# Inverse-spectral tables of a two-layer S5/H3 kernel: TensorE and PSUM copies in place of two transposing DMA transfers, with a new written order

## The chip, the cores and the metric

The kernel runs on one core of a Trainium2 chip. The metric is the device time of one execution in microseconds. A profiled execution gives a trace of its own; its span (first to last instruction) is some two microseconds shorter than the device time of the same execution. Engines are named as in the profile: PE (TensorE matmuls), PEld (its weight loads), DVE (VectorE), ACT (ScalarE), POOL (GpSimd) and SP (the queue that issues nearly all transfers).

## The reference, cut to what matters

A sequence `x` of 2048 tokens with 640 channels goes through four residual layers, A, B, A, B. The two A layers share their weights, and so do the two B layers.

```
x = x + A(layernorm(x)); x = x + B(layernorm(x))      # and the same two once more
A(x): h[t] = lam * h[t-1] + Bbar x[t]   (complex diagonal, 640 states)
      y = 2 Re(C h) + x * Dskip
B(q): k_shift = causal convolution of k with 4 taps;  kv = k_shift * v
      y = irfft(rfft(kv) * rfft(ssm_k))[:2048] + kv * ssm_D      # per channel, length 4096
      returns q * y
```

In layer B only `q` depends on `x`. So `y` of layer B, the long convolution, is computed once from the inputs and used twice.

## The kernel before, in words

**Convolution.** It is a transform of length 4096 written as matmuls with tables of sines and cosines. The 640 channels are taken in five blocks of 128, `yq0` to `yq4`. Each block has these steps, which are the names in the written order:

- `kl`, `ka`, `KA`, `KB`: load the filter, add the skip term, first stage (four groups `m0` to `m3` of matmuls, L1098, each with a copy `e0` to `e3` out of PSUM) and second stage (five groups, L1122 to L1127, with the tables `Cf`, `Sf` and `NSf`);
- `vl`, `VA`, `VB`: the same two stages for `kv`, which `kv_lk`, `kv_lv`, `kv_mm` (L1062) and `kv_ev` (L1068) make;
- `pw`: the pointwise complex product of the two spectra, four DVE instructions (L1175 to L1178);
- `IB`: the first inverse stage, five groups of matmuls (L1197, L1198) with the tables `Ci`, `Si` and `NSi`, each with a copy;
- `tt`: a transposing transfer from arena to arena (L1210); `IA`: the second inverse stage (L1225); `st`: the store to the DRAM scratch `ysd`.

**Tables.** `yt_sin` makes `Cf` and `Sf` on ACT (three groups of up to six of the 17 frequencies, 128 columns each), `yt_neg` makes `NSf`. The inverse tables hold the same blocks, each of them transposed: `yt_Ci` and `yt_Si` are one transposing transfer each (L882, issued by SP) of 17 blocks of 128x128 bf16, and `yt_nsi` negates `Si` on DVE (L886).

**A layers.** Four chunks `c0` to `c3` of 512 tokens each, in each of `A1` and `A2`. Per chunk: layernorm (`ln_bn` for A1, `ln_nm` and `ln_sq` for A2), normalised rows `id`, a transposing transfer `tu`, input products `bq` (L658) and `bp` (L673, L675) with copies `eq` and `ev`, rotation `ri` (L690, L691), two scans `sc` (L707), carry `cy`, rotation back `ro`, `hx` (L732), output products `cp` (L755, four per chunk) and their copies with the residual, `xe` (L763 on ACT for A1, L767 on DVE for A2). The B layers have per chunk a load `l` of `ysd`, layernorm, `u`, a product `mm` (L812) and a sum `m` (L818, L820); the last one stores the output, `st` (L783). The weights of A are made by the `a_` steps.

**Order.** Each step is a task. The string `ORDER` lists all tasks, and `Sched.run` emits them in this order; each engine then works through its own instructions in that order and waits by semaphores for what they need. A suffix `/a`, `/d` or `/p` gives the engine, ACT, DVE or POOL, of a step that has a choice. `evac` (L254 on ACT, L256 on DVE) is the copy out of PSUM. The table `PLACE` gives every buffer its offset in one arena of SBUF and every PSUM tile its first bank out of eight; a buffer that overlaps an older one waits for the older one's last reader.

Of the kernel before, what the change touches and what calls it, by code (L numbers as in the profile page):

```python
# [51 lines left out]
ARENA = 3216  # L52

ORDER = """
    warm yt_io6 kv_kd a_ldB1 a_pl kv_pd1/p kv_pd3/p kv_pd2/p yt_io0 yt_ph6 yt_f0 kv_dsl yt_ph0 yt_sin6 a_ldB0 yt_io12 kv_pd0/p yt_f2 yq0_kl yt_ph12
    yt_sin0 a_p0 kv_d0 a_b01:3 kv_k0 kv_lk0 a_b00:2 a_b0e1:3/d kv_k1 a_b00:3 a_b0e0:2/d kv_d1 yt_f3 a_b0e0:3/a kv_k2 a_p1 yt_f4 a_b00:4 yt_sin12 a_p2
    a_b01:2 kv_lv0 yt_neg6 a_ti a_b01:4 yt_h0 yq0_ka a_b0e1:2/d kv_d2 a_b0e1:4/d yq0_KA:m2 kv_ds0 yq0_KA:m3 a_b0e0:4/a yq0_KA:e2/d yq0_KA:m1 a_p3 yq1_kl
    yq0_KA:m0 kv_ds1 yt_neg12 kv_mm0:0 yt_neg0 yq0_KA:e1/a yq0_KA:e0/d kv_ds2 yq0_KA:e3/a a_p4a kv_lv1 a_p4 a_b00:1 a_p5a yq0_KB:m1 a_b0e0:1/a kv_ds3
    kv_ev0:0 a_ta kv_mm0:1 yq0_KB:e1/d kv_ds4 yq0_KB:m4 kv_lk1 a_b00:0 yq1_ka kv_ev0:1 a_p5b yq0_KB:m0 yt_h1 a_b0e0:0/d yq0_KB:m2 yq0_vl yq0_KB:e4/a a_t0
    yq0_KB:e0/a a_b01:0 a_b01:1 yq0_KB:e2/a a_b0e1:1/a a_p6 a_ldC0 a_t1 a_b0e1:0/d kv_mm1:1 a_lamd kv_mm1:0 a_ldC1 kv_ev1:1 a_b10:1 kv_ev1:0 yq0_VA:m2  # L60
    yq0_KB:m3 a_b1e0:1/d yt_Si yq0_VA:m3 yq0_VA:e2/a yq0_KB:e3/d yq1_KA:m1 yq0_VA:e3/a yq0_VA:m0 yq1_KA:e1/d a_b11:4 yq0_VA:e0/a yq0_VA:m1 yq1_KA:m2
    a_b1e1:4/a yq0_VA:e1/d a_b10:4 yt_Ci yq1_KA:e2/a yq1_KA:m3 yq0_VB:m3 a_b1e0:4/a yq1_KA:e3/d yt_h2 yq0_VB:m0 yq0_VB:e3/a yt_h3/p yq1_KA:m0 a_b10:0
    yq0_VB:e0/d yq1_KA:e0/a yq0_VB:m1 yq1_vl a_f a_b1e0:0/a a_ct1 yq0_VB:e1/a yq0_VB:m2 yt_nsi a_wc01:0 a_b11:0 kv_lk2 yq0_VB:m4 a_wm01:0 a_b1e1:0/a
    yq0_VB:e2/d a_wc01:1 a_b11:3 yq0_VB:e4/a xl0 a_wm01:1 a_b1e1:3/a yq1_KB:m2 yq0_pw yq1_KB:m3 yq1_KB:e2/a yq1_KB:m0 kv_lv2 yq1_KB:e3/a yq1_KB:m1
    yq1_KB:e0/a a_b10:2 a_b11:1 yq1_KB:e1/a a_b11:2 kv_lk3 a_b1e1:1/a a_b10:3 a_b1e1:2/a yq1_VA:m3 kv_pd4/p a_b1e0:3/a kv_mm2:1 yq1_VA:e3/a kv_lv3
    yq1_VA:m0 a_b1e0:2/a kv_ev2:1 yq0_IB:m3 yq1_VA:e0/a yq0_IB:m0 yq0_IB:e3/d kv_mm2:0 yq0_IB:e0/a yq2_kl yq1_VA:m2 yq0_IB:m1 kv_ev2:0 yq1_VA:e2/a
    yq0_IB:m4 yq0_IB:e1/a A1c0_ln_bn:2/d yq1_VA:m1 yq2_vl a_ct0 yq1_VA:e1/a yq0_IB:e4/d yq0_IB:m2 A1c0_ln_bn:0/d a_wc00:0 yq1_VB:m0 a_t2 yq1_KB:m4
    a_wm00:0 yq1_VB:e0/a yq0_IB:e2/d a_wc00:1 yq1_VB:m1 yq1_KB:e4/a A1c0_ln_bn:3/a a_wm00:1 yq0_tt kv_mm3:0 yq1_VB:e1/d a_ct4 kv_ev3:0 a_ct2 a_wc04:0
    a_wc02:0 a_wm04:0 yq1_VB:m3 a_wm02:0 a_wc04:1 a_wc02:1 a_wm04:1 yq1_VB:e3/a a_wm02:1 yq1_VB:m2 yq2_ka kv_lv4 yq2_KA:m3 yq2_KA:m0 yq1_VB:e2/d kv_mm3:1
    yq2_KA:e3/a yq2_KA:e0/a yq1_VB:m4 yq2_KA:m2 kv_ev3:1 a_dd yq1_VB:e4/a yq2_KA:e2/a yq2_KA:m1 kv_lk4 yq1_pw yq2_VA:m2 yq2_KA:e1/a yq2_VA:m3 yq2_VA:e2/a  # L70
    xl2 yq2_VA:e3/a yq2_VA:m0 yq2_KB:m0 yq2_VA:e0/a yq2_KB:m2 yq2_KB:e0/a a_ct3 yq2_KB:e2/a yq2_KB:m4 yq3_kl yq0_IA:m0 a_wc03:0 yq2_KB:m1 yq0_IA:e0/a
    a_wm03:0 yq2_KB:e1/a yq1_IB:m3 yq3_vl yq2_KB:e4/d a_wc03:1 A1c0_ln_bn:1/d yq1_IB:m4 kv_mm4:1 yq1_IB:e3/a a_wm03:1 yq1_IB:e4/a yq1_IB:m1 kv_ev4:1
    yq2_VA:m1 yq0_IA:m1 yq1_IB:e1/a yq2_VA:e1/d yq4_kl yq1_IB:m2 yq1_IB:m0 yq0_IA:e1/d yq1_IB:e2/a yq2_VB:m1 yq1_IB:e0/d A1c0_ln_sd kv_mm4:0 yq3_ka
    yq2_VB:e1/d yq1_tt yq2_VB:m0 kv_ev4:0 yq2_KB:m3 yq2_VB:e0/a yq2_VB:m2 A1c0_ln_post yq2_KB:e3/a A1c2_ln_bn:1/d yq2_VB:m3 yq2_VB:e2/a A1c0_id:3/d
    yq2_VB:m4 yq3_KA:m1 A1c0_id:2/d yq2_VB:e3/a yq2_VB:e4/d yq3_KA:m2 A1c0_id:0/d yq3_KA:m3 yq3_KA:e1/a A1c0_id:1/d yq3_KA:m0 yq2_pw A1c0_tu yq3_KA:e2/a
    yq3_VA:m2 yq3_KA:e3/a yq3_KA:e0/a yq1_IA:m0 yq3_VA:e2/a yq3_KB:m4 yq0_st yq1_IA:m1 yq1_IA:e0/a yq3_KB:m1 yq1_IA:e1/a yq3_KB:m3 xl1 yq3_KB:e1/a
    yq3_VA:m3 A1c0_bq:2 yq3_KB:e4/a yq3_KB:e3/a yq3_VA:e3/d yq2_IB:m2 yq1_st A1c0_eq:2/a A1c2_ln_bn:3/d yq2_IB:m4 yq2_IB:m3 yq2_IB:e2/a yq2_IB:e4/d
    yq2_IB:m1 A1c2_ln_bn:2/d yq2_IB:e3/a yq4_vl yq3_VA:m1 yq3_KB:m0 A1c1_ln_bn:2/d yq2_IB:e1/a yq2_IB:m0 yq3_VA:e1/a A1c1_ln_bn:1/d yq3_KB:m2 yq2_IB:e0/a
    A1c2_ln_bn:0/d A1c0_bp:2 yq3_KB:e2/a yq2_tt A1c1_ln_bn:3/d A1c2_ln_sd yq3_VA:m0 A1c0_bq:1 A1c0_ev:2/a A1c2_ln_post yq3_KB:e0/a A1c2_id:3/d yq4_ka
    A1c1_ln_bn:0/d yq3_VA:e0/a yq4_KA:m3 A1c2_id:1/d yq4_KA:m0 A1c0_eq:1/a yq3_VB:m2 yq4_KA:e3/d yq4_KA:e0/a yq3_VB:m1 A1c2_id:2/d A1c2_id:0/d A1c1_ln_sd  # L80
    yq3_VB:e2/a yq3_VB:m3 A1c2_tu yq3_VB:e1/d yq3_VB:m0 A1c1_ln_post yq3_VB:m4 A1c0_bp:1 yq3_VB:e0/a A1c1_id:2/d A1c1_id:0/d yq3_VB:e4/d yq3_VB:e3/a
    A1c1_id:3/d xl3 A1c1_id:1/a yq3_pw yq4_KA:m1 A1c0_bq:0 A1c0_ev:1/a A1c1_tu yq4_KA:e1/a yq4_KA:m2 A1c2_bq:2 A1c0_eq:0/a yq2_IA:m1 A1c0_bp:0 yq2_IA:e1/a
    yq4_KA:e2/a A1c2_eq:2/d yq2_IA:m0 A1c0_xr A1c0_ev:0/a yq3_IB:m1 yq2_IA:e0/a A1c2_bp:2 A1c0_ri yq3_IB:e1/a A1c1_bq:0 A1c2_ev:2/a yq4_KB:m2 yq3_IB:m3
    A1c0_sc yq4_KB:e2/a yq3_IB:m2 yq3_IB:e3/a yq4_KB:m3 A1c1_eq:0/a A1c1_bq:1 yq3_IB:e2/a yq4_KB:e3/a yq3_IB:m4 yq4_KB:m1 A1c1_eq:1/a yq3_IB:e4/d
    yq3_IB:m0 A1c3_ln_bn:1/a yq4_KB:e1/d A1c1_bq:2 A1c3_ln_bn:3/d A1c2_bq:0 yq3_IB:e0/a A1c0_cy A1c0_ro A1c1_eq:2/a yq3_tt yq4_KB:m4 yq4_KB:m0 A1c2_eq:0/a
    A1c1_bp:0 yq4_KB:e0/a yq4_KB:e4/d A1c1_bp:2 A1c3_ln_bn:2/d A1c1_ev:0/a yq4_VA:m2 yq4_VA:m0 yq2_st A1c1_ev:2/d A1c1_bp:1 yq4_VA:e0/a A1c3_ln_bn:0/d
    yq4_VA:e2/a yq4_VA:m1 yq4_VA:m3 A1c1_ev:1/d A1c2_bp:0 yq4_VA:e1/a A1c1_ri yq4_VA:e3/a A1c2_bq:1 A1c2_ev:0/a A1c3_ln_sd yq4_VB:m3 A1c2_eq:1/a A1c0_hx
# [748 lines left out]
def y_table_tasks(S, nc, wp, St, consts):  # L836
# [43 lines left out]
    for a, b in (("Ci", "Cf"), ("Si", "Sf")):  # L880
        def e_tr(_, a=a, b=b):
            nc.sync.dma_start_transpose(out=T[a].get(), in_=T[b].get().rearrange("p q k -> p (q k)"))  # L882
        t_tr.append(S.add(f"yt_{a}", "sp", 3.5, sins, e_tr, xt=2.8, uses=[T[a], T[b]]))

    def e_nsi(_):
        nc.vector.tensor_scalar(T["NSi"].get(), T["Si"].get(), -1.0, None, ALU.mult)  # L886
# [494 lines left out]
```

## Time and profile before

| what | value |
|---|---|
| median of 3 runs | 350.53 us (350.0 to 350.71) |
| the profiled execution as a run | 350.02 us |
| its span | 348.2 us |
| PE busy | 310.0 us (89%) |
| DVE busy | 326.5 us (94%) |
| ACT busy | 256.3 us (74%) |
| DMA, mean over the span | 120 GB/s; 20 transposes from arena to arena, 5 from DRAM |

Busy time is the time in which at least one instruction of the engine is shown as running; since instructions overlap at their ends, it is less than the sum of their durations. A group of instructions is given with its line, engine and shapes, its count, its busy time with the mean duration of one, and the engine's idle time just before them with what ended it. Lines are those of the kernel before.

### The profile page before, as it was taken

Reading aid. Unit: us, or ns where it says so; the run is one execution under the profiler, and the core shown is the slowest. Engines: PE = TensorE matmul, PEld = TensorE weight load, DVE = VectorE, ACT = ScalarE, POOL = GpSimd, SP = SyncE. Lnnn points to the kernel's source line nnn. Section 1 sums busy time; section 2 is a strip of 40 time slices with the busy share of each in tenths; the row PEclk is TensorE's granted clock in tenths of the full one; section 3 lists DMA queues with packets and bytes.
Section 4 is the critical chain, followed back from the end, with each engine's and each line's share of the span. In section 5 each row is a group of like instructions: output and inputs, shape, how many; then the busy total and the mean of one; then the engine's idle time right before and its main releaser. Section 6 shows DMA issues by size and latency. Waiting matters only on the chain.

```text
span 348.2 us, 9466 instructions
## 1 busy us (share of the span) xinstructions
PE 310.0 (89%) x4110; PEld 248.4 (71%) x4110; DVE 326.5 (94%) x449; ACT 256.3 (74%) x411; POOL 20.6 (6%) x62
## 2 busy tenths in 40 slices
PE   7777897779799999999999999999999999998910
PEld 7665887768698899896666786876877787654500
DVE  8999898899999989798999999999999999999996
ACT  6999898797998768566867689897776856008850
POOL 5690000010000000000000000000000000000000
PEclk9999999899999999999999999999999999999975
DMA  8999999887999920800259642315009500000024
GB/s 231 218 170 257 186 228 154 167 185 152 180 230 179 218 77 10 174 2 0 77 120 215 189 177 52 100 18 130 6 5 227 135 15 2 0 2 0 3 112 188
DMA packets 105868, 41.71 MB, mean 120 GB/s; under 512 B 98141, under 2 KB 100706, under 8 KB 105826
## 3 DMA queue, kind: packets, MB, share of 16 engines
q1 hardware_dynamic: 105680, 41.10, 53.7%
q8 instruction: 32, 0.52, 0.6%
q14 instruction: 10, 0.08, 0.1%
q10 hardware_dynamic: 146, 0.01, 0.0%
HBM read 19.02 MB, written 5.24 MB: 70 GB/s over the span
## 4 chain that ended last, share of the span: by engine, by line
PE 62%; DVE 27%; ACT 6%; issue 3%; POOL 0%; DVEq 0%; ACTq 0%; POOLq 0%
PE banks L755 18%; PE banks L658 11%; PE banks L673 11%; ACT arena L254 5%; DVE arena L256 3%; DVE arena L690 3%; DVE arena L707 3%; DVE arena L820 3%; DVE arena L767 3%; PE banks L1197 2%; PE banks L1198 2%; PE banks L675 2%; PE banks L1098 2%; PE banks L1289 2%; PE banks L1122 2%
## 5 line engine op out<-in xcount | busy, mean ns | idle before, releaser
L254 ACT ACTIVATE arena<-banks 128x1024 bf16<-128x1024 f32 (+4 forms) x150 | 129.5, 929 | 31.9 <-PE banks L658 9.2
L755 PE MATMUL banks<-arena 128*128 128x128 bf16 (+1 forms) x800 | 101.0, 283 | 1.7 <-DVE arena L767 1.7
L755 PEld LDWEIGHTS <-arena 128*128 128x128 bf16 x800 | 60.6, 98 | 41.7 <-issue 1.9
L673 PE MATMUL banks<-arena 128*128 128x256 bf16 x400 | 53.2, 273 | 0.0
L256 DVE CAST arena<-banks 128x1024 bf16<-128x1024 f32 (+4 forms) x43 | 41.7, 979 | 5.6 <-PE banks L675 2.5
L658 PE MATMUL banks<-arena 128*128 128x256 bf16 x400 | 46.2, 273 | 0.0
L690 DVE TENSOR_TENSOR arena<-arena 128x5160 bf16<-128x5160 bf16 x16 | 45.5, 2844 | 0.4
L707 DVE TENSOR_TENSOR_SCAN arena<-arena 128x1290 bf16<-128x1290 f32 x16 | 44.7, 2833 | 0.3
L673 PEld LDWEIGHTS <-arena 128*128 128x128 bf16 x400 | 38.6, 98 | 4.6
L658 PEld LDWEIGHTS <-arena 128*128 128x128 bf16 x400 | 38.5, 98 | 4.7
L555 ACT ACTIVATE junk<-arena,nmean 128x640 bf16<-128x640 f32 x48 | 39.7, 827 | 1.3
L1122 PE MATMUL banks<-arena 128*128 128x128 bf16 x170 | 35.5, 221 | 4.6 <-DVE arena L427 1.5
L1125 PE MATMUL banks<-arena 128*128 128x128 bf16 x170 | 35.7, 221 | 0.0
L1127 PE MATMUL banks<-arena 128*128 128x128 bf16 x150 | 33.2, 221 | 0.0
L1124 PE MATMUL banks<-arena 128*128 128x128 bf16 x150 | 33.2, 221 | 0.0
L609 ACT ACTIVATE arena<-arena,nmr,rstd 128x640 bf16<-128x640 f32 (+1 forms) x32 | 27.8, 912 | 5.8 <-DVE nmr L568 3.8
L691 DVE TENSOR_TENSOR arena<-arena 128x2580 bf16<-128x2580 bf16 x16 | 24.1, 1504 | 0.5
L675 PE MATMUL banks<-arena,ident_bf 128*128 128x256 bf16 x80 | 21.8, 273 | 0.0
L763 ACT ACTIVATE arena<-banks 128x640 f32<-128x640 f32 x15 | 10.4, 697 | 14.0 <-PE banks L755 14.0
L1197 PE MATMUL banks<-arena 128*128 128x128 bf16 x160 | 19.6, 219 | 0.7 <-ACT arena L254 0.5
L1198 PE MATMUL banks<-arena 128*128 128x128 bf16 x160 | 19.4, 219 | 0.3 <-DVE arena L1178 0.3
L1124 PEld LDWEIGHTS <-arena 128*128 128x128 bf16 x150 | 14.8, 99 | 5.1 <-issue 5.1
(196 smaller groups left out, 498.8 us busy)
## 6 DMA issues: line engine op xcount, KB each, us to landing
arena<-in_A_x_dram SPq DMA_DIRECT2D x8, 640.0 KB, 5.5
arena<-ysd SPq DMA_DIRECT2D x8, 640.0 KB, 5.9
arena<-in_B_ssm_k_dram SPq DMA_DIRECT2D x5, 512.0 KB, 7.7
arena<-in_B_v_dram SPq DMA_DIRECT2D x5, 512.0 KB, 6.3
ysd<-arena SPq DMA_DIRECT2D x5, 512.0 KB, 4.5
out_dram<-arena SPq DMA_DIRECT2D x8, 320.0 KB, 2.2
arena<-in_A_B_im_dram SPq DMA_DIRECT2D x1, 800.0 KB, 5.2
arena<-in_A_B_re_dram SPq DMA_DIRECT2D x1, 800.0 KB, 7.1
```

The lines of the kernel that those rows point to most:

```text
L254: nc.scalar.activation(out, in_, ACT.Copy)
L256: nc.vector.tensor_copy(out, in_)
L555: nc.scalar.activation(small.junk, src(q), ACT.Square, bias=st["nmean"][:, i:i + 1], scale=1.0, accum_out=st["ssq"][:, i:i + 1])
L658: nc.tensor.matmul(pq[:, jj, c2, :], lhsT=bt0[:, c2, k, j * P:(j + 1) * P], rhs=uT[:, 2:4, k, :], start=(k == 0), stop=(k == NJ - 1))
L673: nc.tensor.matmul(pb[:, jj, c2, :], lhsT=bt1[:, c2, j, k, :], rhs=uT[:, 0:2, k, :], start=(k == 0), stop=False)
L690: nc.vector.tensor_tensor(tt, gs[:, :, None].to_broadcast([P, 2, 2, n]), by_pairs(w["tab"].get().rearrange("p i j b -> p (i j b)"), n), AL ...
L707: nc.vector.tensor_tensor_scan(gv, rt, gv, 0.0, ALU.mult, ALU.add)
L755: nc.tensor.matmul(pc[:, o0:o1], lhsT=lh, rhs=rh, start=(n == 0), stop=(n == len(ops) - 1))
L1122: nc.tensor.matmul(ps[:, g, 0, :], lhsT=T["Cf"].get()[:, q, :], rhs=are, start=True, stop=single)
L1124: nc.tensor.matmul(ps[:, g, 0, :], lhsT=T["Sf"].get()[:, q, :], rhs=A[:, 2 * q + 1, :], start=False, stop=True)
L1125: nc.tensor.matmul(ps[:, g, 1, :], lhsT=T["NSf"].get()[:, q, :], rhs=are, start=True, stop=single)
L1127: nc.tensor.matmul(ps[:, g, 1, :], lhsT=T["Cf"].get()[:, q, :], rhs=A[:, 2 * q + 1, :], start=False, stop=True)
```

## The change

`yt_Ci`, `yt_Si` and `yt_nsi` go. In their place stand fifteen smaller tasks. For `Cf` and for `Sf`, the 17 blocks are taken in groups of 8, 8 and 1. Each group is multiplied by the identity, block by block, with the block as weights, so that the transposed blocks stand in PSUM (`yt_tCf0`, `yt_tCf8`, `yt_tCf16`, the same for `Sf`; 34 matmuls in all). From there `Ci` (from `Cf`), `Si` and, with a factor of -1, `NSi` (both from `Sf`) are copied to the arena by ACT or DVE (`yt_eCi0` and so on, nine copies of 1024, 1024 and 128 columns). What needed the three old steps needs all nine copies.

`ORDER` is written anew throughout, with the same other tasks; 80 steps that have a choice of ACT or DVE stand on the other one than before, and three small memsets go from POOL to DVE. `PLACE` is new throughout as well, with places in PSUM for the six new tiles, and the arena is 3212 units in place of 3216. The new tasks stand in the order together, after yq1's `KB:e0` and before yq0's `IB`:

```
... yq1_KB:e0/a yt_tCf8 kv_lk3 a_b10:2 a_b1e1:2/a yt_tSf0 yt_eCi8/a yt_tSf8 yt_eNSi0/a a_b1e0:2/d xl0
yt_eSi0/a yt_eNSi8/d yt_tCf0 kv_mm2:0 yt_eCi0/a yt_eSi8/d yt_tSf16 yt_tCf16 kv_lv3 yt_eNSi16/a yq1_VA:m3
yt_eCi16/d yt_eSi16/a kv_ev2:0 yq1_VA:m0 kv_mm2:1 yq1_VA:e3/a yq1_VA:e0/a yq1_VA:m2 yq0_IB:m3 ...
```

The diff of the code, without `ORDER` and `PLACE`:

```diff
-    t_tr = []
-    for a, b in (("Ci", "Cf"), ("Si", "Sf")):
-        def e_tr(_, a=a, b=b):
-            nc.sync.dma_start_transpose(out=T[a].get(), in_=T[b].get().rearrange("p q k -> p (q k)"))
-        t_tr.append(S.add(f"yt_{a}", "sp", 3.5, sins, e_tr, xt=2.8, uses=[T[a], T[b]]))
-
-    def e_nsi(_):
-        nc.vector.tensor_scalar(T["NSi"].get(), T["Si"].get(), -1.0, None, ALU.mult)
-    K["inv"] = t_tr + [S.add("yt_nsi", "dve", 0.65, t_tr, e_nsi, uses=[T["NSi"], T["Si"]])]
+    inv = []
+    for b, outs in (("Cf", (("Ci", 1.0),)), ("Sf", (("Si", 1.0), ("NSi", -1.0)))):
+        for g0 in range(0, NQ, 8):
+            n = min(8, NQ - g0)
+            s_pt = S.bank(f"it{b}{g0}", (n + 3) // 4)
+
+            def e_tm(_, b=b, g0=g0, n=n, s_pt=s_pt):
+                for q in range(n):
+                    nc.tensor.matmul(s_pt.get()[:, q * P:(q + 1) * P], lhsT=T[b].get()[:, g0 + q, :], rhs=consts["ident_bf"][:], start=True, stop=True)
+            t_tm = S.add(f"yt_t{b}{g0}", "pe", c_mm(P, n), sins, e_tm, uses=[s_pt, T[b]])
+            for a, sc in outs:
+                def e_te(eng, a=a, sc=sc, g0=g0, n=n, s_pt=s_pt):
+                    o, i = T[a].get()[:, g0:g0 + n, :].rearrange("p q k -> p (q k)"), s_pt.get()[:, 0:n * P]
+                    if eng == "act":
+                        nc.scalar.activation(o, i, ACT.Copy, scale=sc)
+                    else:
+                        nc.vector.tensor_scalar(o, i, sc, None, ALU.mult)
+                inv.append(S.add(f"yt_e{a}{g0}", ("act", "dve"), (c_act(n * P), c_tt(n * P, True)), [t_tm], e_te, uses=[s_pt, T[a]]))
+    K["inv"] = inv
```

## The prediction

> **What bounds the kernel now.** I read three views in this order: busy time by stretch, the timeline around the two places where the stretches change, and the groups of instructions by shape. First the stretches. The columns are PE, PEld, DVE, ACT and POOL busy time with the number of instructions, then the granted clock, the DMA share and GB/s.
>
> ```profile
> 10.00:43.20 33.20, 24.87 (x606) 21.93 (x604) 31.74 (x58) 32.06 (x52) 13.77 (x38) 1.00 1.14 206
> 43.20:98.40 55.20, 45.92 (x1084) 41.59 (x1082) 51.24 (x64) 47.98 (x62) 1.83 (x5) 0.97 0.93 179
> 98.40:281.90 183.50, 183.50 (x1933) 144.96 (x1933) 173.04 (x221) 141.31 (x238) 0.00 (x0) 1.00 0.46 109
> 281.90:332.00 50.10, 48.16 (x409) 32.35 (x407) 49.51 (x58) 24.58 (x43) 0.00 (x0) 1.00 0.03 10
> 332.00:348.20 16.20, 0.00 (x0) 0.00 (x0) 12.87 (x22) 3.81 (x12) 0.00 (x0) 0.61 0.35 133
> ```
>
> There are three regimes. Up to 98.4 us DVE and ACT carry the load (DVE 91 to 96% busy) and PE has holes. From 98.4 to 281.9 us PE has no hole, while DVE leaves 10.5 us empty. From 281.9 us DVE is full to the end, and after 332 us it is alone. The chain of waits says the same: PE pieces from 98.38 (L658) to 281.11 us, then DVE pieces only. The second view shows the joints.
>
> ```profile
> 25.74 10.76 SPq L882 DMA_TRANSPOSE arena<-arena  x2
> 94.46 0.64 PE L1225 MATMUL banks<-HA,arena 128*128 128x64 bf16 x16 [1.65 <-DMA arena<-arena]
> 281.87 0.69 DVE L256 CAST arena<-banks 128x512 bf16<-128x512 f32 x1 [0.41 <-PE banks L675]
> ```
>
> The first line is what the change removes: two transposes that hold SP's queue for 10.76 us. The second is the last hole of PE, a wait for another transpose (yq1_tt, which stays). The third is where DVE takes over: it waited 0.41 us for A2c2_bp:2. Third, the groups that price the new work (busy, mean ns of one, idle before):
>
> ```profile
> L254 ACT ACTIVATE arena<-banks 128x1024 bf16<-128x1024 f32 x112 | 109.6, 1033 | 30.6 <-PE banks L658 9.2 <-PE banks L1127 7.9 <-PE banks L675 5.6
> L256 DVE CAST arena<-banks 128x1024 bf16<-128x1024 f32 x25 | 30.3, 1220 | 3.8 <-PE banks L1127 1.6 <-PE banks L675 1.5 <-PE banks L1098 0.3
> L419 PE MATMUL banks<-ident_bf,arena 128*128 128x128 bf16 x50 | 3.8, 219 | 0.9 <-issue 0.9
> L886 DVE TENSOR_SCALAR arena<-arena 128x2176 bf16<-128x2176 bf16 x1 | 0.7, 718 | 0.0
> ```
>
> **What the Trainium skill says.** "VectorE: DVE Perf Modes", section "The three transpose paths", gives 390 ns for a 128x128 bf16 transpose on TensorE, which ends in PSUM, and 1309 ns on the DMA path, which ends in SBUF. In this trace an identity matmul lasts 219 ns, and ten of L419 take 0.72 us, so one costs about 55 ns of PE. In bulk the two transfers took 10.76 us for 34 blocks, 316 ns each. The page's point that counts is the destination: out of PSUM somebody must copy. "Perfetto Trace Analysis", section "Optimizing Scalar/DVE Operations", advises moving work to Scalar when DVE is saturated; here a copy of 1024 columns costs 1033 ns on ACT and 1220 on DVE, and neither has much room before 98 us. The same page, "Identifying the Most-Contended Engine", warns that matmul busy time is no measure of headroom. I checked it: ten 256-column matmuls of L658 take 1.09 us, 109 ns each, and PE's instructions from A1c0_bq:2 to A2c2_bp:2 priced in this way add up to 183.0 us, against 182.7 measured. So PE really is at its pace there.
>
> **The change, part by part.** All sums price the two written orders with the rows above.
>
> 1. *Removed:* two transfers and yt_nsi (0.72 us of DVE). No engine's wait in the list of waits up to 70 us names a DMA, except waits of the queue itself; the first product of the inverse stage (L1197) starts at 50.1 us and waits for DVE's product and for ACT. So the freed 10.76 us of SP and the data they moved lie beside other work. The most that it could give back is PE's one wait for a DMA, the 1.65 us shown at 94.46. A loss is excluded, since less is moved. I take 0.
>
> 2. *Added on PE:* 34 matmuls of 55 ns, 1.9 us. They stand before kv_mm2 and yq1_VA, in the regime where PE has 9.3 us of holes (55.20 - 45.92). Between 0 and 1.9; I take 0, but they count in the positions below.
>
> 3. *Added copies:* Ci, Si and NSi, each 1024 + 1024 + 128 columns. The order puts four large and two small on ACT (4 x 1.03 + 2 x 0.30 = 4.7 us) and two large and one small on DVE (2 x 1.22 + 0.27 = 2.7 us). The small ones lie below the 256-column rows (about 0.41 us). A scaled copy from PSUM on DVE (the NSi one) isn't in the trace; bounds are 1.03 and 1.3 us, I take 1.22.
>
> 4. *The added wait:* yq0_IB:m3 now waits for all nine copies. Between yq0_pw and it stand 5.3 us more of ACT's work. Queued behind it on PE are the other inverse products, yq1_VA:m1 and yq1_KB:m4, and yq0_tt waits for them. But the order has moved other work ahead: before yq0_tt stand only 1.4 us more on ACT and 0.8 us on DVE. I take nothing apart for it; if PE ran dry there, it would be up to 5.3 us.
>
> 5. *New order and engines.* Over the whole program some 80 copies and normalisations change engine, almost in balance: +0.9 us on DVE, +0.3 on ACT. With parts 1 to 3 DVE has 2.0 + 0.9 = 2.9 us more, ACT 5.0, PE 1.9. Where it falls matters:
>  - Up to yq0_pw: DVE -0.9, ACT 0. Nothing taken.
>  - Up to yq2_pw (91.73 us now): DVE +3.2. This is tables +2.0, three bn_stats steps of A1's chunk 2 brought forward +3.5 (3 x 1.16), a_t2 put later -1.2, exchanged copies -1.1. ACT has +5.4. DVE has 3.3 us of holes in 43.2 to 71.2 us and 0.6 in 71.2 to 91.7. I assume that about a third of the former is filled (1.0): yq2_pw and A1c0_tu come 2.2 us later. Bounds: 0 and 3.2.
>  - Behind yq2_pw: DVE -0.3 (2.9 - 3.2).
>  - PE between A1c0_bq:2 and A2c2_bp:2: A2c0_cp:3 (3.0 us) now stands behind A2c2_bp:2, and yq3_VA:m3 (0.5) comes in: -2.5.
>  - From A2c2_ri to the end on DVE: A2c0_xe:3 (0.8) and a small step (0.3) come in, 1.2 us unrounded.
>
> *The loads and stores moved on SP's queue* (yq4_vl and yq0_st later, xl3 and B1l3 earlier, B2l3 behind two stores of the output) have work before their readers: between the last of these stores and the first reader of B2l3 stand about 13 us of DVE work, against 5.9 us to landing of such a load. I take 0. New places in PSUM and the arena: no row prices a clash; half a microsecond either way.
>
> **The sum, two ways.** By PE: A1c0_bq:2 comes 2.2 later (it needs A1c0_tu), then -2.5, then +1.2: +0.9. By DVE: yq2_pw 2.2 later, then 0.3 less work behind it with the same 14.4 us of holes: +1.9. Both must be met, so the larger holds: 348.2 + 1.9 = 350.1 us of span. The profiled execution took 350.02 us as a run and the median is 350.53, so the time is 350.53 + 1.9 = **352.4 us**. This case's own range is 351.3 to 353.8.
>
> **The rivals.**
> - *The new copies fall into holes, and the order gains (faster).* For it: 3.9 us of holes on DVE and 7.2 on ACT in 43 to 91.7 us, 9.3 on PE, and a freed SP queue that lets x and k be loaded earlier, which is why bn_stats can come forward. Against: ACT and DVE were both over 95% busy before 43 us. If yq2_pw isn't later at all, PE gives 0 - 2.5 + 1.2 = -1.3 and DVE -0.3 with the holes of DVE behind it shrinking by 1.0: 350.53 - 1.3 = 349.2. It decides if A1c0_bq:2 starts by about 98.8 us of span.
> - *Hidden both ways (same).* The copies are absorbed as far as PE's -2.5 pays for: 350.5.
> - *The chain on PE breaks (slower still).* PE from 98 us has no hole now; in the new order it waits once more for a transpose as at 94.46 (1.65 us), and no hole of DVE takes the 2.9: +4.5, 355.0. For it: 183 us without a hole leaves nothing to gain and much to lose.
> - *The change doesn't do what it says:* excluded; the changed program's instructions have two DMA transposes fewer and the nine copies.
>
> **How the numbers follow.** Forecast 352.4: 0.41. Faster, 349.2: 0.34. Same: 0.13. Slower still, 355.0: 0.12. A measurement can tell about 0.2%, 0.7 us, from no change. Faster by more 0.34, within 0.13, slower 0.53. The range from 348.0 to 355.4 reaches to both outer cases with 1.2 us below the one and 0.4 above the other for the places.
>
> **What would show it.** Rows: L886 gone; ACT's 128x1024 copies at 115 in the helper and 4 from the tables, DVE's at 22 and 2; 18 transposes from arena to arena in place of 20. DVE's busy time near 329.4, ACT's 261, PE's 312. yq2_pw (third L1175-type step) near 94 us; the first A1 product (L658-type) near 100.6 instead of 98.38; DVE's takeover near 281.6. I am wrong if yq2_pw starts before 92.5 us, or if DVE's holes fall by over 3 us.

## The result and the profile after

The changed kernel takes 356.17 us (355.7 to 356.7, 3 runs) against 350.53 us before: ratio 1.0165, interval 1.0136 to 1.0194. A second comparison of the same two kernels, listed below, gave 355.15 against 350.31 us, ratio 1.0132 (1.0106 to 1.0158). So the change makes the kernel about 5 us slower. The forecast was 352.4 us with a range of 348.0 to 355.4: the sign was right, the size too small, and the first comparison lies 0.8 us above the range. The span is 353.9 us (before 348.2). All ratios leave out two disturbed executions (1115 us of B_order_alone, 361 us of W_order_bn_act) and are estimates over all other executions, not quotients of the medians, so the two can differ by some 0.2%.

The stretches up to the first product of layer A, cut at the three pointwise steps `yq0_pw`, `yq1_pw` and `yq2_pw`, show where the time goes. First the kernel before; the columns are window, length, then PE, PEld, DVE, ACT and POOL busy with counts, clock (the share of its full speed that PE was granted, so 0.50 is half clock), DMA share and GB/s; times are in microseconds.

```profile
0.00:43.17 43.17, 32.44 (x690) 29.44 (x691) 39.83 (x88) 38.62 (x58) 18.77 (x57) 1.00 1.08 211
43.17:71.28 28.11, 23.54 (x574) 21.46 (x572) 24.79 (x34) 23.28 (x34) 1.83 (x5) 0.94 1.01 185
71.28:91.73 20.45, 18.03 (x426) 16.49 (x426) 19.88 (x28) 18.04 (x22) 0.00 (x0) 1.00 0.83 174
```

The same view of the kernel after, with the long PE stretch and the tail in the last two lines:

```profile
0.00:44.70 44.70, 35.31 (x695) 31.67 (x696) 39.43 (x91) 38.63 (x57) 17.66 (x54) 0.92 0.90 193
44.70:73.96 29.26, 22.77 (x529) 20.61 (x528) 26.40 (x35) 24.48 (x33) 7.39 (x5) 1.00 0.90 161
73.96:98.40 24.44, 21.35 (x493) 19.82 (x489) 22.70 (x32) 21.53 (x27) 0.00 (x0) 0.86 0.66 115
104.70:286.50 181.80, 181.75 (x1915) 143.43 (x1915) 170.90 (x213) 135.80 (x226) 0.00 (x0) 1.00 0.47 108
286.50:353.90 67.40, 51.06 (x435) 34.22 (x432) 63.69 (x84) 32.20 (x64) 0.00 (x0) 0.91 0.14 50
```

The three lengths grow by 1.5, 1.2 and 4.0 us, so `yq2_pw` starts 6.7 us later. I call the second and third line of each fence the first and the second convolution stage. ACT's busy time in the two grows by 4.69 us (24.48 + 21.53 - 23.28 - 18.04), DVE's by 4.43, and the length of the two stages together by 5.14. From 104.7 us PE is full again (181.75 of 181.80 us).

The groups of the kernel after (busy, mean ns of one, idle before):

```profile
L256 ACT ACTIVATE arena<-banks 128x1024 bf16<-128x1024 f32 x115 | 112.5, 1030 | 22.9 <-PE banks L660 5.9 <-PE banks L677 5.4 <-PE banks L1110 5.0
L258 DVE CAST arena<-banks 128x1024 bf16<-128x1024 f32 x22 | 26.6, 1218 | 6.5 <-PE banks L677 3.1 <-PE banks L1110 1.6 <-PE banks L1139 1.0
L889 PE MATMUL banks<-ident_bf,arena 128*128 128x128 bf16 x34 | 2.6, 219 | 2.1 <-DVE arena L258 2.1
L895 ACT ACTIVATE arena<-banks 128x1024 bf16<-128x1024 f32 x4 | 3.9, 1075 | 0.7 <-PE banks L889 0.7
L897 DVE TENSOR_SCALAR arena<-banks 128x1024 bf16<-128x1024 f32 x2 | 2.3, 1209 | 0.0
```

The counts are those forecast (115 and 4, 22 and 2), and so are the prices: a table copy of 1024 columns takes 1075 ns on ACT (1033 assumed) and 1209 on DVE (1220 assumed, the row that wasn't in the trace of before).

Last, the timeline of the kernel after at the joints (start, length, engine, instruction, idle before it and its releaser):

```profile
58.13 1.95 SPq L1173 DMA_TRANSPOSE arena<-arena  x1
60.59 0.23 PE L1209 MATMUL banks<-arena 128*128 128x128 bf16 x1 [1.97 <-issue]
104.75 1.25 PE L660 MATMUL banks<-arena 128*128 128x256 bf16 x10 [0.90 <-DMA arena<-arena]
286.88 0.68 DVE L258 CAST arena<-banks 128x512 bf16<-128x512 f32 x1
```

A1c0_bq:2 starts at 104.75 us (before 98.31), DVE takes over at 286.88 (before 281.87). So the whole loss of span, 5.7 us, is +6.4 up to A1c0_bq:2, -1.4 in PE's long stretch (183.5 to 182.1) and +0.7 in the tail (66.3 to 67.0). The second line is a stop of PE whose cause the profile doesn't name; the last section returns to it.

### The profile page after: what moved, and what is told of

Read it like the earlier page. It is cut to its first block, busy times and chain, and to the rows that moved or that the text cites. A ratio compares the mean times of both kernels' runs of the same rounds, so it can differ in the third digit from the quotient of the medians.

```text
span 353.9 us, 9537 instructions
## 1 busy us (share of the span) xinstructions
PE 316.3 (89%) x4144; PEld 253.5 (72%) x4144; DVE 329.3 (93%) x456; ACT 259.0 (73%) x411; POOL 25.1 (7%) x59
## 5 line engine op out<-in xcount | busy, mean ns | idle before, releaser
L256 ACT ACTIVATE arena<-banks 128x1024 bf16<-128x1024 f32 (+4 forms) x149 | 129.3, 932 | 33.9 <-PE banks L660 12.4
L757 PEld LDWEIGHTS <-arena 128*128 128x128 bf16 x800 | 60.5, 98 | 40.8 <-issue 1.0
L660 PEld LDWEIGHTS <-arena 128*128 128x128 bf16 x400 | 38.5, 98 | 5.6 <-issue 1.0
L675 PEld LDWEIGHTS <-arena 128*128 128x128 bf16 x400 | 38.7, 98 | 4.7
L611 ACT ACTIVATE arena<-arena,nmr,rstd 128x640 bf16<-128x640 f32 (+1 forms) x37 | 32.0, 913 | 11.3 <-DVE arena L693 6.3
L1110 PEld LDWEIGHTS <-arena 64*128 64x128 bf16 x320 | 10.2, 97 | 10.7 <-issue 8.0
```

Source lines behind the costliest of these rows:

```text
L256: nc.scalar.activation(out, in_, ACT.Copy)
L660: nc.tensor.matmul(pq[:, jj, c2, :], lhsT=bt0[:, c2, k, j * P:(j + 1) * P], rhs=uT[:, 2:4, k, :], start=(k == 0), stop=(k == NJ - 1))
L675: nc.tensor.matmul(pb[:, jj, c2, :], lhsT=bt1[:, c2, j, k, :], rhs=uT[:, 0:2, k, :], start=(k == 0), stop=False)
L757: nc.tensor.matmul(pc[:, o0:o1], lhsT=lh, rhs=rh, start=(n == 0), stop=(n == len(ops) - 1))
```

## The experiments

The quoted texts are what was expected of a run, written before it.

| kernel | median us (before, same chip) | ratio (interval) | starts of `yq0_pw`, `yq1_pw`, `yq2_pw`, A1c0_bq:2 | span |
|---|---|---|---|---|
| C_after_again: the kernel after | 355.15 (350.31) | 1.0132 (1.0106-1.0158) | 44.1, 74.6, 98.3, 104.6 | 353.8 |
| A_tables_alone | 356.67 (350.18) | 1.0206 (1.0165-1.0247) | 43.0, 77.4, 97.8, 104.4 | 354.1 |
| B_order_alone | 353.28 (350.18) | 1.0087 (1.0058-1.0117) | | |
| F_order_pool | 353.34 (349.71) | 1.0100 (1.0071-1.0129) | 43.4, 71.6, 95.2, 100.5 | 350.4 |
| E_pool_moved | 354.21 (350.18) | 1.0113 (1.0083-1.0144) | 43.9, 73.1, 96.7, 103.3 | 352.4 |
| H_work_only | 356.17 (349.71) | 1.0197 (1.0164-1.0229) | 43.7, 76.2, 98.8, 106.7 | 356.6 |
| L_act_only | 357.12 (350.81) | 1.0177 (1.0147-1.0207) | 44.8, 77.1, 98.0, 106.2 | 356.1 |
| I_matmuls_only | 352.50 (349.71) | 1.0079 (1.0056-1.0102) | 43.3, 71.8, 92.5, 100.7 | 350.6 |
| K_six_copies | 353.61 (349.71) | 1.0107 (1.0083-1.0131) | 43.7, 74.5, 98.1, 103.4 | 353.0 |
| D_bn_back | 359.11 (350.18) | 1.0242 (1.0204-1.028) | 45.1, 77.4, 101.0, 107.3 | 358.8 |
| V_pool_bn_act | 359.38 (350.31) | 1.0247 (1.0204-1.029) | 43.4, 74.2, 99.2, 105.2 | 358.2 |
| W_order_bn_act | 356.95 (350.31) | 1.0168 (1.0142-1.0195) | 43.3, 70.0, 95.0, 100.2 | 354.1 |
| P_work_filled | 358.27 (350.81) | 1.0219 (1.0188-1.0249) | 44.4, 77.3, 98.8, 106.4 | 356.3 |
| N_pool_filled | 355.53 (350.81) | 1.0152 (1.011-1.0195) | 43.6, 75.7, 99.4, 107.9 | 357.2 |
| Q_before_filled | 350.71 (350.81) | 0.9995 (0.9979-1.0012) | 43.2, 69.1, 89.9, 97.9 | 348.3 |
| Z_before_filled2 | 349.75 (349.78) | 0.9992 (0.9978-1.0007) | 43.1, 69.5, 91.0, 97.9 | 347.9 |
| R_loads_later | 355.20 (350.31) | 1.0134 (1.0109-1.0159) | 43.3, 73.4, 97.4, 103.7 | 352.7 |

The starts belong to the one profiled execution of each kernel, which as a run lay up to 2.2 us above the median (H) or 1.2 below it (F), and 3.5 above for N. One regularity holds across the table: span less start of A1c0_bq:2 is 249.9 us before, and 249.0 to 250.4 in every kernel but D, V and W, where work was moved behind that point (251.5, 253.0, 253.9). Whatever the change costs is thus lost before layer A starts.

Two things help in reading the single traces. The first stage differs from execution to execution by up to 3 us where the order up to `yq1_pw` is the same: 29.3, 30.5 and 32.2 us (after, C, D), 29.2 and 30.9 (E, V), 28.1 and 26.7 (F, W). The second stage hardly differs: 23.64 or 23.65 us in C, D, E, F, K and N, 24.99 in V and W; R took 23.96, and the first trace of the kernel after 24.44.

The expectations missed often: A, D, H, I, L, N, V and W took longer than any time named for them.

**Which half costs: the tables or the order?** A puts the new table steps into the old order, B and F leave the transfers and take only the new order and engines. F has E's moves on POOL as well (below).

```diff
A, against before:
-  yt_Si   -  yt_Ci   -  yt_nsi
   ... a_b1e1:2/a
+  yt_tCf8 yt_tSf0 yt_eCi8/a yt_tSf8 yt_eNSi0/a yt_eSi0/a yt_eNSi8/d yt_tCf0 yt_eCi0/a yt_eSi8/d
+  yt_tSf16 yt_tCf16 yt_eNSi16/a yt_eCi16/d yt_eSi16/a
B, against after:
-  all fifteen table steps
   ... a_ldC1
+  yt_Si yt_Ci
   ... a_b1e0:2/d
+  yt_nsi
F: B and the POOL moves of E
```

> Before's order and places, with the two transfers and yt_nsi taken out and the 34 matmuls and nine copies put in one block behind a_b1e1:2, on the engines that after uses. If the copies are what costs (T1): DVE carries 2.0 us and ACT 4.7 us more before yq2_pw, where both are full, so yq2_pw moves from 91.7 to 94 us or later and the time is 352.5 to 356. If the new order costs (T2): the time stays within 0.7 us of before, 350 to 351. If slow stretches of TensorE's clock before 84 us cost (T3): no stretch at half speed at 15 to 21 us, so at most 351.5.

> After's order and places, with the two transposing transfers and yt_nsi (behind a_ldC1 and behind a_b1e0:2; the slots of Si and NSi exchanged) in place of the matmuls and copies. T1: without the copies yq2_pw comes back towards 92 to 95 us, time 350 to 352.5. T2: yq2_pw stays near 97 to 98 us and the time at 355 to 356.5, as the order keeps its holes. T3: the clock dips at 15 to 21 us stay, those at 76 to 83 us may go; 352 to 355.

> After's order with the two transfers, as in B_order_alone, and GpSimd's work moved as in E_pool_moved. If the 3.1 us that B costs are mostly GpSimd's place (E gave some 1.8 us back): 350.8 to 352. If B's cost is the rest of the order (bn_stats brought forward, waits for banks): 352.5 to 354, as B. The profile, which B lacks, shows yq1_pw and yq2_pw without copies: near 70 to 71.5 and 92 to 95 us.

Both halves cost. By the ratios, on 350.5 us, A loses 7.2, B 3.0 and F 3.5; with the tables on top of F's order the loss is 4.0 (E), on top of B's 4.6 to 5.8 (C and the first comparison). The tables cost 7.2 us in the old order and 0.5 (E less F) to 2.8 (V less W, below) in the new one, which has by itself cost 3.0 to 3.5 already. B's one trace is of an execution of 1115 us and isn't used; F's stretches show where the order loses:

```profile
43.43:71.57 28.14, 21.35 (x495) 19.72 (x494) 24.38 (x33) 20.00 (x26) 0.00 (x0) 0.94 1.06 180
71.57:95.22 23.65, 20.51 (x494) 18.84 (x489) 22.42 (x33) 21.38 (x27) 0.00 (x0) 0.93 0.60 127
```

The first stage is as long as before (28.14 against 28.11) with 3.3 us less ACT work in it (20.00 against 23.28). That work is not saved: the second stage holds 3.3 us more of it (21.38 against 18.04) and is 3.2 us longer. The order has cleared a place for the copies by pushing work of the convolution over `yq1_pw`: ACT's, but PE's and DVE's as well (20.51 against 18.03 us and 22.42 against 19.88 in the second stage), so F doesn't show which engine's share counts. With the tables in that place, E's first stage has ACT 24.55 busy and is 1.0 us longer than F's; V's is 4.2 longer than W's (30.85 against 26.65), with the same orders up to there.

The trace of F shows one more thing in the second stage, which no run isolates:

```profile
79.10 2.21 ACT L280 ACTIVATE arena<-banks 128x1024 bf16<-128x1024 f32 x3 [1.63 <-DVE arena L1204]
```

ACT waits here for the last instruction of `yq1_pw`, 7.53 us after that step's start. The copy is `yq2_KB:e0`. In the new `PLACE` its target `yq2_SK` (136 units from 1608) lies over `yq1_SV` (136 units from 1568), which `yq1_pw` reads; before, the two lie apart (2608 and 3080). ACT waits in this way for 1.35 to 1.67 us in every trace of the new order but R's, and in none of the old one. No run moves the buffer, so how much of the 3.2 us comes from this overlap, and how much from the order, stays open.

**Is it the placement beside GpSimd, or the bn_stats brought forward?** E moves what POOL does around `yq0_pw` to earlier or later places. D puts three bn_stats of A1's chunk 2 and two small steps back behind `yq2_pw`.

```diff
E, against after:
   kv_ds1
+  kv_ds3 kv_ds2 kv_ds4        (each taken from its later place)
   ... a_b10:4
+  yt_h2 yt_h3/p
   ... yq2_KA:e2/a
+  a_dd
D, against after:
-  A1c2_ln_bn:1/d A1c2_ln_bn:3/d A1c2_ln_bn:0/d A1c2_ln_sd A1c2_ln_post   (ahead of yq2_IB:m3)
+  A1c2_ln_bn:3/d behind A1c0_eq:2, :1/d behind yq2_IB:m1, :0/d, ln_sd and ln_post behind yq2_IB:m3
```

> After, with GpSimd's work moved away from the small DVE steps: kv_ds2, kv_ds3 and kv_ds4 up behind kv_ds1, yt_h2 and yt_h3 in front of a_f, a_dd down to yq1_pw, where before has it. If GpSimd's placement lengthens a_f (2.7 us for 1.4) and holds up yq0_pw and what follows: yq0_pw 1 to 1.5 us earlier, near 43.5 us, and the time 354.5 to 355.5. If it is only beside: within 0.7 us of after, 355.5 to 357.

> After, with three bn_stats of A1 chunk 2 (3 x 1.16 us of DVE) and its sqrt and post step put back behind yq2_pw, as before has them. If the work brought forward costs (part of T2): yq2_pw about 3.5 us earlier, near 95 us, A1c0_bq:2 near 101 us, time 352.5 to 354, less than 3.5 gained only if DVE runs dry behind it or PE then waits. T1 alone (copies): the same shift of yq2_pw, but the 3.5 us of DVE come back behind it; 355 to 356.

E's interval overlaps both comparisons of the kernel after, so a gain from it isn't separated. `yq0_pw` started at 44.1 to 45.1 us in the three kernels with POOL as in the change and at 43.3 to 43.9 in seven with E's moves. But kernels with before's order up to there range from 43.0 to 44.8 as well (A, L), so I count 0 to 1.8 us for this, and nothing as shown.

The bn_stats theory (that the DVE work brought forward is what costs) falls. Stretches of D, second convolution stage and the one behind it up to `yq3_pw`:

```profile
77.35:100.99 23.64, 20.42 (x493) 18.73 (x489) 19.90 (x23) 21.43 (x26) 0.00 (x0) 0.93 0.67 117
100.99:126.82 25.83, 21.50 (x345) 19.10 (x345) 24.02 (x45) 20.72 (x27) 0.00 (x0) 1.00 0.87 179
```

and the same two of E:

```profile
73.07:96.71 23.64, 20.53 (x494) 18.86 (x489) 22.41 (x32) 21.32 (x27) 0.00 (x0) 0.93 0.69 117
96.71:120.31 23.60, 21.15 (x345) 19.04 (x345) 20.95 (x36) 20.82 (x26) 0.00 (x0) 1.00 0.96 196
```

The second stage takes 23.64 us with DVE busy for 19.90 or 22.41: taking 2.5 us from DVE there gains nothing, and behind it the same work costs 2.2 us (25.83 against 23.60). So DVE's sum, on which the prediction built, doesn't set this stage. D loses more in all than this shows: its first stage was 32.24 us, with the same order up to there as after.

**What of the tables costs: ACT's time, DVE's, or PE's?** H adds to the kernel before copies of the same number of columns on ACT (4 x 1024, 2 x 128) and three instructions of 2176 columns on DVE, into unused places, in one block; nothing waits for them. L adds ACT's part alone. I adds only the 34 matmuls, whose result nobody reads.

```diff
H, against before:
   ... a_b1e1:2/a
+  dm_a0 dm_a1 dm_a2 dm_d0 dm_a3 dm_d1 dm_a4 dm_d2 dm_a5
L: +  dm_a0 dm_a1 dm_a2 dm_a3 dm_a4 dm_a5
I: +  yt_tCf8 yt_tSf0 yt_tSf8 yt_tCf0 yt_tSf16 yt_tCf16
```

> Before, whole, with nothing but work of the copies' size put behind a_b1e1:2: ACT four copies of 1024 and two of 128 columns, DVE three of 2176 (0.72 us each), from an SBUF table into unused places; no matmul, no PSUM, no wait, and nothing reads the results. If the cost of the tables is the time on two full engines: ACT's 4.7 us come out at 3.5 to 4.7, time 353.5 to 355. If it is PE starved and clocked down behind the PSUM banks that the copies hold: at most 352. As the prediction took it (a third hidden, 2.2): 352 to 352.8.

> Before, whole, with the 34 matmuls put where A has them, into the same PSUM banks, and no copies; nothing reads the banks. 1.9 us of PE's time in a stage where PE has holes: within 0.7 us of before, 349.5 to 351. If PE's work there is on the path: up to 352.

> H_work_only with ACT's part alone (four copies of 1024 and two of 128 columns, 5.05 us in H's trace), without the three steps on DVE. If ACT is the engine that counts there: nearly all of H's 6.5 us, time 354.5 to 356. If DVE is: at most 352. If both share: 352.5 to 354.5.

L is the sharpest run of the study. With six more instructions of ACT, with no reader and no new wait, the kernel takes 6.2 us more, as with H (6.9) and nearly as with the real tables in the same place (A, 7.2); the intervals overlap. The timeline of L (ACT's copies out of PSUM are L281 here) shows how:

```profile
50.00 5.05 ACT L919 ACTIVATE arena<-arena 128x1024 bf16<-128x1024 bf16 x6
54.95 3.10 ACT L281 ACTIVATE arena<-banks 128x640 bf16<-128x640 f32 x4
55.69 0.61 PE L1131 MATMUL banks<-FV,arena 64*128 64x128 bf16 x8 [4.27 <-ACT arena L281]
```

and so do its stretches, two short ones and the first stage:

```profile
52.00:54.70 2.70, 0.00 (x0) 0.00 (x0) 1.30 (x2) 2.61 (x4) 0.00 (x0) 0.96 1.27 241
54.70:60.00 5.30, 4.01 (x50) 3.65 (x51) 1.23 (x1) 3.54 (x7) 0.00 (x0) 0.50 0.34 55
...
44.76:77.11 32.35, 24.55 (x574) 22.30 (x572) 24.56 (x34) 27.50 (x40) 1.83 (x5) 0.89 0.84 135
```

The block holds ACT's queue for 5.05 us. The copy out of PSUM that PE's next product waits for stands behind it, so PE is empty for 4.27 us, DVE is half empty (1.30 of 2.70 us), and when PE resumes it runs at half clock for 5.3 us. The first stage is 4.24 us longer (32.35 - 28.11) for 4.22 us more of ACT. ACT was only 83% busy in this stage before, with 4.83 us idle; after the block it still has 4.85 us idle. The holes moved, they didn't fill.

This stage, with 0.45 us in the next, is not the whole loss of L's trace, whose span is 7.9 us longer: 1.6 us stand ahead of `yq0_pw`, before the block is reached, where L has half clock from 30.6 us on, and 1.6 behind `yq2_pw`, with half clock (below). What the block is shown to cost is therefore 4.2 to 4.7 us, about ACT's added time. That is a block at one place of the old order; no run puts the same work elsewhere or in pieces.

Holes stay in the other kernels too: in the eighteen traces ACT's in the first stage are 3.3 us (Q) to 8.1 (F), in the second 1.9 (R) to 5.9 (V and W). In the first stage of before and of L over 4 us of them are waits for PE's products, and PE's waits there end on copies of ACT and DVE. "Perfetto Trace Analysis", section "Optimizing Scalar/DVE Operations", in the Trainium skill suggests offloading to Scalar when DVE is saturated. L takes nothing from DVE, so it doesn't test the advice, but it shows its limit here: Scalar was less busy than DVE (23.28 against 24.79 us of 28.11), and its idle time was no room for the block.

I costs 2.8 us, where the prediction took 0 for the matmuls. In its profiled execution `yq2_pw` is 0.7 us later and A1c0_bq:2 2.3 us; the 1.6 us in between come with half clock (below). How much this adds where the copies are there too isn't known.

**Do fewer copies help?** K makes `NSi` from `Si` by one DVE instruction, as before, so that six copies remain; ACT has 1.25 us less, DVE 0.5.

```diff
K, against E:
-  yt_eNSi0/a   -  yt_eNSi8/d   -  yt_eNSi16/a
   ... yt_eSi16/a
+  yt_nsi
```

> E_pool_moved with six copies in place of nine: NSi comes from Si in one step on DVE (0.72 us), as before has it, in place of 1.03 + 0.2 us on ACT and 1.2 us on DVE. If copy time on ACT and DVE is what costs: 1.0 to 1.5 us less than E, time 352.7 to 353.3. If the wait for the last table costs more (NSi now waits for all of Si): no better than E, 354 to 355.

No difference from E (1.0107 and 1.0113). The first product of the inverse stage comes 0.8 us earlier (56.26 against 57.09), and a longer stop of PE follows (1.71 us against 0.98). Both kernels have one half-clock stretch in this stage, K at 60 us and E at 53. The copies that were saved stand in a stage that varies by more than their time, so K can't price them.

**Does spare DVE time help ACT in the second stage?** V moves three copies of this stage from ACT to DVE and the bn_stats behind it as in D, so that DVE has room; W does the same without the tables.

```diff
V, against E; W, against F:
-  yq2_KB:e1/a  yq1_IB:e1/a  yq2_VB:e0/a
+  yq2_KB:e1/d  yq1_IB:e1/d  yq2_VB:e0/d
   and the bn_stats as in D
```

> E_pool_moved with the three bn_stats steps behind yq2_pw (as in D_bn_back) and three of ACT's copies of the stage between yq1_pw and yq2_pw (yq2_KB:e1, yq1_IB:e1, yq2_VB:e0) given to DVE in their stead. That stage took 23.64 us in D, E, F and K alike, with and without 3.5 us of bn_stats on DVE. If ACT sets it: 2 to 3 us shorter, near 21 us, time 351.5 to 353. If DVE or PE's order sets it: still 23 to 24 us, time 353.5 to 355.

> The same two edits in F_order_pool (after's order, transfers in place of the tables). If ACT sets the stage: 350 to 351.5, as fast as before. If not: as F, 352.5 to 354.

The second stage of V:

```profile
74.21:99.20 24.99, 20.43 (x494) 18.74 (x489) 23.13 (x26) 19.06 (x23) 0.00 (x0) 0.93 0.65 116
```

ACT is 2.3 us less busy than in E and the stage is 1.35 us longer; W's is 24.99 us too. So the theory that ACT's sum sets this stage falls too. Neither engine's sum does. The waits fit a chain that alternates between PE, ACT and DVE, in which a copy out of PSUM on DVE costs more (1218 against 1030 ns) and stands behind other DVE work; no run shows the chain link by link.

V and W also price the tables in the new order a second time, beside each other: 1.0247 less 1.0168, or 2.8 us, with an interval of some 1.8 us either way.

**Is PE's clock the cause?** In the traces half-clock stretches follow short stretches in which PE is nearly empty. Q and Z fill them in the kernel before, P and N in H and E, by issuing some groups of matmuls again into the same place.

```diff
+REP = {"yq1_VB:m3": 2}                          # Q, on before
+REP = {"yq1_VB:m3": 2, "yq3_VA:m2": 4}          # Z, on before
+REP = {"kv_mm2:1": 4}                           # P, on H
+REP = {"yt_tSf8": 4, "yq2_KA:m2": 2, "yq2_KA:m3": 2, "yq2_VA:m2": 2, "yq2_KA:m1": 2}   # N, on E
-                t.emit(...)
+                for _ in range(REP.get(nm, 1)):
+                    t.emit(...)
```

> Before, whole, with the 16 matmuls of yq1_VB:m3 issued twice: 0.9 us more of PE work at 64.4 us, in its wait of 1.52 us there. If that wait brings the half clock at 66 to 69 us, and that lies on the path (DVE and ACT wait for PE there): clock 1.0, and 0.7 to 1.5 us less than before, 348.5 to 349.5. If not: within 0.7 us of before.

> Q_before_filled with a second group issued again: yq3_VA:m2 four times, 1.2 us of work in PE's wait of 1.43 us at 91 us, which stands ahead of a stretch at half clock (94 to 97 us) in Q. Q had yq2_pw 1.9 us earlier than before and lost it in that stretch. If the half clock follows from PE's empty time and takes the gain: A1c0_bq:2 near 96 us and the time 348 to 349.3, faster than both kernels. If not: 350 to 351.5, as Q.

> H_work_only with the 64 matmuls of kv_mm2:1 issued four times instead of once (the same values each time): they fill PE's wait of 4.28 us in front of yq1_VA:m0, where it stood idle, with 3.3 us of work whose result isn't wanted before. If the half clock behind that wait (54.6 to 61 us) costs time: the clock stays at 1.0 there, and 2 to 3 us come back, 353 to 354.5. If the clock is beside the path: as H, 355.5 to 357, or later by what the repeats hold up.

> E_pool_moved with PE's groups ahead of its waits at 50 and 74 us issued again: yt_tSf8 four times (1.8 us, in the wait of 1.83 us for a_b1e0:2), yq2_KA:m2, m3, m1 and yq2_VA:m2 twice each. If the two stretches at half clock (52 to 57, 76 to 81 us) cost: they are gone and 1.5 to 3 us come back, 351 to 352.7. If not: as E, 353.5 to 355.

Two stretches of the kernel before:

```profile
64.40:66.00 1.60, 0.08 (x2) 0.05 (x1) 1.53 (x3) 1.60 (x3) 0.00 (x0) 0.98 1.09 205
66.00:69.30 3.30, 3.30 (x60) 3.10 (x61) 2.05 (x3) 1.59 (x2) 0.22 (x1) 0.50 0.40 90
```

and of Q:

```profile
64.40:66.00 1.60, 0.96 (x18) 0.84 (x16) 1.59 (x2) 1.60 (x2) 0.00 (x0) 1.00 1.84 162
66.00:69.30 3.30, 2.97 (x110) 2.45 (x109) 2.75 (x5) 2.61 (x5) 1.83 (x5) 1.00 0.57 127
```

With the filler the half-clock stretch is gone, PE does 110 instead of 60 matmuls in the second window, and `yq1_pw` comes 2.1 us earlier. Yet the time is the same (Q 0.9995, Z 0.9992): A1c0_bq:2 starts at 97.9 instead of 98.3 us. Q loses its gain between `yq2_pw` and A1c0_bq:2. Before:

```profile
91.73:98.31 6.58, 4.29 (x91) 3.58 (x85) 6.51 (x5) 6.58 (x8) 0.00 (x0) 1.00 0.92 171
```

and in Q, with two matmuls more, at a mean clock of 0.79:

```profile
89.85:97.92 8.07, 5.83 (x93) 5.20 (x87) 7.34 (x5) 7.69 (x10) 0.00 (x0) 0.79 0.99 203
```

This piece takes 7.6 to 8.2 us in the five traces of the old order that have half clock in it (H, I, L, P, Q) and 6.6 to 7.0 in the three that haven't (before, A, Z). So a half-clock stretch goes with 1.0 to 1.6 us here. Z has none in this place, but one in its second stage, and then waits 0.3 us for the transfer A1c0_tu.

The kernel after has no half clock in this piece, in either of its traces. In the second stage of the new order N shows what its removal gains:

```profile
75.74:99.39 23.65, 19.56 (x519) 18.11 (x513) 22.42 (x33) 21.48 (x27) 0.00 (x0) 1.00 0.59 117
```

At full clock, and with 25 matmuls more, the stage is as long as at 0.93 in C, F and K (23.65 us). At 0.86 the kernel after took 24.44, so half clock may have cost it 0.8 us there, not the 4.0. In the first stage the question stays open: P and N ran into PE's own stops of 3.2 and 3.7 us, and both are no faster than H and E. The kernel after lost 1.2 us in that stage at full clock.

**Is it the stop of PE at 60 us?** R moves two loads, `kv_lk3` and `kv_lv3`, later on SP's queue.

```diff
R, against E:
-  kv_lk3  -  kv_lv3
   ... yq2_vl
+  kv_lk3 kv_lv3
```

> E_pool_moved with two loads (kv_lk3, kv_lv3) moved on SP's queue behind yq2_vl, that is from about 48 and 52 us to 60. PE stood without a visible reason in front of its 988th or 989th matmul in every kernel of the old order until 55.6 to 56.3 us and of the new one until 59.5 to 62.4. If that is something that PE needs and that comes behind the loads in the DMA queues: it ends by 57.5 us, 1 to 2 us gained, 352 to 353.5. If the loads have nothing to do with it: the wait stays near 59.7, time as E or up to 1 us more (kv_mm3 waits).

> After itself, beside the others, so that what GpSimd's place costs is read on one chip: if it is 1.8 us (E against after), after is at 1.015 to 1.018 of before here, and E's variants lie 0.005 lower. Its own PE wait at the 988th matmul again near 60 us.

The stop goes. PE's waits in R show one for a moved load instead (us in total, count, longest):

```profile
PE banks L1099 <- DMA arena<-in_B_k_dram: 2.0, 1, 2.0
```

R has the time of the kernel after run beside it (1.0134 and 1.0132), so nothing is gained. C itself lies below what was expected of it (1.015 to 1.018), so the 1.8 us for GpSimd's place aren't confirmed. No kernel of the study is faster than the one before; Q and Z equal it.

## Why the prediction was right or wrong

- **The frame held.** One sum of the prediction starts from how late A1c0_bq:2 comes, the other from `yq2_pw`. PE's long stretch gave -1.4 (forecast -2.5) and the tail +0.7 (forecast +1.2). With +6.4 in front these make the 5.7 us of span. From `yq2_pw` to the end the kernel after takes 1.0 us less (forecast -0.3). Of the busy times DVE's came as worked out (329.3, forecast 329.4); ACT's grew by 2.7 us, not 5, and PE's by 6.3, not 2.
- **The step that failed is step 5's term "up to `yq2_pw`".** It put: DVE +3.2, about a third of the first stage's holes filled, 2.2 us later, bounds 0 and 3.2. Measured: 6.7 us later, over twice the upper bound. DVE had 4.0 us more work by then, ACT 4.7. The term took DVE's sum for the pace, and D shows that it is not. DVE's holes didn't fill either: up to `yq2_pw` they grew from 7.2 to 9.9 us. ACT's +5.4 stood beside it in the same line and was counted at nothing, with 7.2 us of holes there. L shows that this can't be done: 5.05 us of ACT in one block, 4.83 us idle in that stage, 4.2 us lost in it. That is the tables' side, and in the old order.
- **The new order at nothing but engine counts** failed in the same term: B and F lose 3.0 to 3.5 us without any table, and up to `yq2_pw` F has hardly more ACT work than before (80.27 against 79.94 us). A sum up to `yq2_pw` hides what crosses `yq1_pw`, and the new places were put at "half a microsecond either way" without asking which buffers overlap. What in the order or the places costs the 3.2 us of the second stage isn't shown. The line on `yq0_pw`, where nothing was taken, was off too, by 1.5 us (in C by 0.95).
- **Step 4 (the added wait).** It took nothing and named 5.3 us as the end if PE ran dry. The first inverse product comes 12.4 us after `yq0_pw` (57.10 against 44.70), before 7.0 (50.14 against 43.17): 5.4 later, so at this place the upper end came in. Measured in the same way 3.9 us are left at `yq0_tt` and 1.2 at `yq1_pw`, so most of it was made up, and it isn't a further term beside step 5's.
- **Step 3 (prices)** was right within about 4% for the large copies, and nothing speaks against **step 1**: taking the transfers out gained nothing that shows (A, without them, takes no less than H, which keeps them; but A has the matmuls as well).
- **Step 2 (34 matmuls at nothing)** was too low: I measured 2.8 us (1.0079, 1.0056 to 1.0102), more than the 1.9 us of PE's time that it gave as the upper bound. In I's trace 0.7 us of it stand at `yq2_pw`; the rest comes with half clock. I can't say how much of it is in the change's loss.
- **The rivals.** "Faster" and "same" assumed that the copies fall into holes, which L speaks against. "The chain on PE breaks", 355.0, is nearest in number, but not for its reason: from 104.7 us PE has no hole, and A1c0_bq:2 waits only 0.90 us for a transfer.

What is shown: the order and places alone lose 3.0 to 3.5 us, the tables add 0.5 to 2.8 us in them, and in the old order a block of ACT's time is enough for most of what the tables cost there. What stays open: why the second stage of the new order takes 23.65 us, and how the tables' part splits between ACT's queue, the added wait, the clock and PE's stops.

## What to carry to other kernels

Idle time of an engine inside a chain need not be room: if its waits end on products of another engine that waits for the first one's copies, new work in its queue can delay the whole chain by its length, and the holes are still there afterwards. Before counting work at nothing because "the engine is 83% busy", look who ends its waits, and what that engine waits for; if it is a loop, let the range reach to the work's full length. An order that makes room has moved something: look for it in the next stage before you call the room free. And when buffers get new places, look for those that now lie over one that is still being read.

## What the runs showed of the hardware that I had not expected

- **PE stops at fixed counts of matmuls, and the end of the stop follows a packet of instructions.** The profile names "issue" as the cause. PE paused at its 476th or 477th matmul in twelve of the eighteen traces (until 29.4 to 30.6 us, for 0.2 to 1.3 us) and at the 988th or 989th, 512 further on, in thirteen, whatever instruction stood there. The second stop lasted 0.9 us before, 2.0 in the change, 3.2 in P and 3.7 in N, and wasn't there in A, H, L, R and W. In the old order it ended between 55.6 and 56.3 us however early PE arrived. The traces also hold the packets of DMA queue q8, which the profile calls "instruction", 16 KiB each. All 25 stops end 1.25 to 1.57 us after one of these has landed: 54.68 and 56.22 us before, 59.20 and 60.59 in the kernel after. In the five traces without the second stop PE reached that matmul 1.5 us or more after the landing. In R, with the two loads later, the packet landed at 55.01 us, in E at 58.32. So these stops are waits for that packet, as far as times can show it.
- **The clock changes in steps of 3.41 us.** Up to layer A every half-clock stretch of the eighteen traces lasted 3.41, 6.83 or 10.24 us. Where the steps lie against the program differs from execution to execution: E and V, with the same order up to `yq1_pw`, had theirs in the first stage at 53.3 and 60.1 us. Such a step of the kernel before and the next:

```profile
62.52:65.93 3.41, 1.49 (x24) 1.25 (x22) 3.34 (x5) 3.14 (x6) 0.00 (x0) 1.00 1.12 215
65.93:69.34 3.41, 3.39 (x61) 3.19 (x62) 2.12 (x3) 1.70 (x3) 0.26 (x1) 0.50 0.41 91
```

  The Trainium skill's "TensorE: Matmul & The Clock Gate", section "Part 1: The HAM clock gate", gives the same two states, half and full, and an idle window of about 3.4 us. The traces agree with its length, and show that PE need not be idle for all of it: it was busy for 1.49 of 3.41 us before this half clock, and for 0.34 in L.
- **The same steps, very different prices.** The same table steps cost 7.2 us in the old order (A less before) and 0.5 to 2.8 in the new one (E less F, V less W, in ratios), with intervals of some 1.5 to 1.8 us either way.
